# Zero-padding copies on another queue, an earlier projection and a reordered start in a two-branch kernel (long filter beside chunked attention)

## The chip, the cores and the metric

The kernel runs on one core of a Trainium2 chip. The metric is the time of one execution on the device in microseconds. An execution is 8865 instructions on five engines: TensorE (PE in the profile, its weight loads PEld), VectorE (DVE), ScalarE (ACT), GpSimd (POOL) and SyncE (SP), which here only issues DMAs. Each engine takes its instructions in the order in which they were compiled and waits at the first one that isn't ready.

## The reference

Two independent branches work on 2048 tokens by 640 channels in bf16, and their results stand side by side in the output.

Branch A is a gated long filter: a short causal filter of four taps on `k`, times `v`, then a causal convolution of each channel with its own filter of length 2048 (given by Fourier transforms), a skip term, and a gate `q`:

```python
for t in range(ks):                                   # ks = 4
    k_shift = k_shift + k_pad[:, t:t + S, :] * shift_k[:, ks - 1 - t][None, None, :]
kv = k_shift * v
y = irfft(rfft(kv, 2 * S) * rfft(ssm_k, 2 * S))[:S]   # per channel
a = q * (y + kv * ssm_D)
```

Branch B is attention with a memory, 32 heads of width 20, in four segments of 512 tokens:

```python
for s in range(4):
    p = softmax(qs @ ks.T * scale + mask)             # causal within the segment
    a_dot = p @ vs
    a_mem = phi(qs) @ M / (phi(qs) @ z + 1e-6)        # memory of the earlier segments
    outs.append(g * a_mem + (1 - g) * a_dot)
    M = M + phi(ks).T @ vs ; z = z + phi(ks).sum(rows)
b = concat(outs) @ wo                                 # q, k, v = x @ wq, x @ wk, x @ wv
```

## The kernel before

**Branch A** works on five blocks of 128 channels, `dp` 0 to 4 (`a_chunks`). The transforms are matmuls with tables of cosines and sines (`Wf` forward, `Wi` inverse, 1 MB each) between butterflies on DVE. For a block: `load_kv` loads v (`vt`) and transposes k from DRAM into `kr` with four DMA transposes (L184), after a memset of its 16 padding columns on POOL (L182), and makes `skd`, the four taps as diagonal matrices (L186, from `ident` and `skc`). `kshift` (L202) applies the short filter with 64 matmuls and multiplies by v (L203). `fwd` (L218, evicted by ACT in L221) and `bfly` transform the product ("X") and the long filter ("K"). `load_sk` loads the long filter (L169), reorders it on DVE (L171) and transposes it by DMA (L175). Then come `pointwise`, the inverse butterfly `ybfly`, and `inverse` (L283, L284), which stores through POOL (L285).

**Branch B** works in eight units `u`: segment u // 2, half u % 2 of the heads (16 heads, in four groups of four).

- `b_proj_chunks(u)` makes the operands of unit u: `xT` by DMA transpose (L301, once for two units), four chunks `proj(t)` of 128 tokens (L312; ACT copies K and Q into one of two tiles `KQ` in L314, and SP transposes these into `KT` and `QT`, L317 and L318), `bound`, and `mem`, which adds to the memory. `bound` finds the greatest magnitude of K (`kam`, L328, which needs all of KT), makes the positive features of Q (`PqT`, L332 to L335, which needs all of QT), takes magnitudes of Q (`qabs`, L337), multiplies them (L340, `pb`), and writes the result bT as one extra row of each head into QT (four DMAs, L345). That row lowers the scores, so that the exponentials need no maximum.
- `b_attn_chunks(u)` is the attention: two `spread` steps copy KT into the zero-padded tiles `KZ[0]` and `KZ[1]` (L377, four DMAs each, one for a head of each group of four), and four `attn(g)` steps use them: scores (L395), exponentials on ACT (L399), the causal mask on DVE (L402), the product with V (L412), the memory's part (L415) and the normalisation on DVE (L418 to L426). `KZ[0]` serves groups 0 and 1, `KZ[1]` groups 2 and 3. There is one `KT` tile, so the next unit's KT waits until both spreads have read this one. After each second unit comes the output projection (`outt`, `outproj`, L441 to L443).

**The order** is a list of chunks with written costs. `merge` interleaves lists so that each goes forward by the same share of its cost: unit u's attention (28.2 in all) with unit u+1's projection (16 to 17.6) and the output projection of earlier units; then this whole list of B with the list of A. Ahead of it stands a start: the projection of unit 0 and the forward part of block 0. The tile framework turns the list into one instruction order per engine; it follows the list as a priority, by modelled readiness, so the compiled order can differ from the list in detail.

**Queues.** SP issues nearly all DMAs, transposes among them, one after the other. POOL issues constants, `Drow` (the skip weights, L173) and all stores. ACT issues three loads at the start (`bt`, two thirds of `w0`, `Wf`), where `w0` and `w1` are the two halves of the projection weights.

Of the kernel before, what the change touches and what calls it, by code (L numbers as in the profile page):

```python
# [10 lines left out]
BF16_NP = ml_dtypes.bfloat16  # L11
bf16 = mybir.dt.bfloat16
# [48 lines left out]
class K3:  # L61
    def __init__(self, ctx, tc, A_q, A_k, A_v, A_shift_k, A_ssm_k, A_ssm_D, B_x, B_wq, B_wk, B_wv, B_wo, B_beta, out):
        self.tc = tc
        nc = self.nc = tc.nc
# [20 lines left out]
        c = self.consts  # L85
        V = nc.vector

        def const(name, arr, dt):
            t = c.tile(list(arr.shape), dt, name=name)
            nc.gpsimd.dma_start(out=t[:], in_=nc.inline_tensor(arr, name="c_" + name).ap())  # L90
            return t

        self.Wf = c.tile([128, 2, 4, 512], bf16, name="Wf")
# [4 lines left out]
        def wload(engs, half):  # L98
            def f():
                for i, (w, eng) in enumerate(zip((B_wk, B_wq, B_wv), engs)):  # L100
                    eng.dma_start(out=self.wqkv[:, :, half, i, :], in_=w.rearrange("(cc p) j -> p cc j", p=128)[:, :, 320 * half:320 * half + 320])
            return f
        self.deferred = {
            "Wf": lambda: nc.scalar.dma_start(out=self.Wf[:], in_=nc.inline_tensor(Wf_np, name="c_wf").ap()),
            "Wi": lambda: nc.sync.dma_start(out=self.Wi[:], in_=nc.inline_tensor(Wi_np, name="c_wi").ap()),
            "w0": wload((nc.scalar, nc.scalar, nc.sync), 0), "w1": wload((nc.sync,) * 3, 1),
            "wo": lambda: nc.sync.dma_start(out=self.wo[:], in_=B_wo.rearrange("(cc p) j -> p cc j", p=128)),
        }
        self.skc = c.tile([128, 5, 4], bf16, name="skc")
        nc.gpsimd.dma_start(out=self.skc[:], in_=self.shift_k.rearrange("(c p) t -> p c t", p=128))  # L110
        self.ident = const("ident", np.eye(128).astype(BF16_NP), bf16)
        bt = self.bt = c.tile([128, H], bf16, name="bt")
        nc.scalar.dma_start(out=bt[:], in_=B_beta.partition_broadcast(128))
        self.sel = const("sel", sel_np, bf16)
# [44 lines left out]
    def a_chunks(self, dp):  # L159
        nc = self.nc  # L160
        V = nc.vector
        dsl = slice(128 * dp, 128 * dp + 128)
        Wf, Wi, ident = self.Wf, self.Wi, self.ident
# [13 lines left out]
        def load_kv():  # L177
            vt = st["vt"] = io.tile([128, 4, 4, 128], bf16, name="vt", tag="vt")
            for b in range(4):
                nc.sync.dma_start(out=vt[:, b], in_=self.v[512 * b:512 * b + 512, dsl].rearrange("(p c) d -> p c d", c=4))  # L180
            kr = st["kr"] = io.tile([128, 4, KPAD + 512], bf16, name="kr", tag="kr")
            nc.gpsimd.memset(kr[:, :, 0:KPAD], 0.0)  # L182
            for c in range(4):
                nc.sync.dma_start_transpose(out=kr[:, c, KPAD:KPAD + 512], in_=self.k[:, dsl].rearrange("(r c) d -> r c d", c=4)[:, c, :])  # L184
# [9 lines left out]
        def kshift(b):  # L194
            def f():
                kr, vt = st["kr"], st["vt"]
                ps = self.bank(self.ps_a, "pks")
                for c in range(4):
                    for t in range(4):
                        cc = (c - t) % 4  # L200
                        p0 = KPAD + 128 * b + (c - t - cc) // 4
                        nc.tensor.matmul(ps[:, 128 * c:128 * c + 128], lhsT=kr[:, cc, p0:p0 + 128], rhs=st["skd"][:, t, :], start=(t == 0), stop=(t == 3))  # L202
                V.tensor_tensor(out=vt[:, b, :, :], in0=ps[:].rearrange("p (c d) -> p c d", d=128), in1=vt[:, b, :, :], op=ALU.mult)  # L203
            return f
# [69 lines left out]
        def inverse(c):  # L274
# [11 lines left out]
            return f  # L286

        X = [(load_kv, 0.1)] + [(kshift(a), 1.5) for a in range(4)] + [(fwd("X", c), 2.0) for c in range(4)] + [(bfly("X"), 7.0)]
        Kc = [(load_sk, 0.1)] + [(fwd("K", c), 2.0) for c in range(4)] + [(bfly("K"), 5.5)]
        Dl = [(load_q, 0.1), (pointwise(0), 4.6), (pointwise(1), 5.0), (ybfly, 7.6)] + [(inverse(c), 1.7) for c in range(4)]  # L290
        return X + Kc, Dl

    def b_proj_chunks(self, u):
        nc = self.nc
# [71 lines left out]
    def b_attn_chunks(self, u):  # L366
        nc = self.nc
# [5 lines left out]
        def spread(gg):  # L373
            def f():
                for hl in range(4):
                    rows = slice(32 * hl, 32 * hl + DH + 1)
                    nc.sync.dma_start(out=self.KZ[gg][rows, :, hl, :], in_=self.KTs[u][rows, 2 * gg:2 * gg + 2, :])  # L377
            return f

        def attn(g):  # L380
# [67 lines left out]
        tail = [(outt, 0.1)] + [(outproj(t), 1.5) for t in range(4)] if half == 1 else []  # L448
# [1 line left out]


def merge(*lists):
    lists = [l for l in lists if l]
    tot = [sum(c for _, c in l) for l in lists]
    done = [0.0] * len(lists)
    idx = [0] * len(lists)
    out = []
    for _ in range(sum(len(l) for l in lists)):
        best = None
        for i, l in enumerate(lists):  # L460
            if idx[i] < len(l):
                v = (done[i] + 0.5 * l[idx[i]][1]) / tot[i]
                if best is None or v < best[0]:
                    best = (v, i)
        i = best[1]
        out.append(lists[i][idx[i]])
        done[i] += lists[i][idx[i]][1]
        idx[i] += 1
    return out


NST, NA, NB, NO = 3, 2, 2, 1


@with_exitstack
def kernel(
    ctx: ExitStack,
    tc: tile.TileContext,
    A_q: bass.AP,
    A_k: bass.AP,  # L480
    A_v: bass.AP,
    A_shift_k: bass.AP,
    A_ssm_k: bass.AP,
    A_ssm_D: bass.AP,
    B_x: bass.AP,
    B_wq: bass.AP,
    B_wk: bass.AP,
    B_wv: bass.AP,
    B_wo: bass.AP,
    B_beta: bass.AP,  # L490
    out: bass.AP,
):
    K = K3(ctx, tc, A_q, A_k, A_v, A_shift_k, A_ssm_k, A_ssm_D, B_x, B_wq, B_wk, B_wv, B_wo, B_beta, out)
    K.xTs, K.o_s, K.oT, K.KTs = {}, {}, {}, {}
    D_ = K.deferred
    A_ = [K.a_chunks(dp) for dp in range(5)]
    a_pro = A_[0][0]
    a_main = []
    for dp in range(5):
        a_main += merge(A_[dp][1], A_[dp + 1][0] if dp < 4 else [])  # L500
    p0 = K.b_proj_chunks(0)
    seq = [p0[0], (D_["w0"], 0), (D_["Wf"], 0), a_pro[0]] + p0[1:4] + [(K.beta_setup, 0)] + p0[4:5] + merge(p0[5:], a_pro[1:] + [(D_["w1"], 0)])
    seq += [(D_["Wi"], 0), (D_["wo"], 0)]
    b_main = []
    tail = []
    for u in range(8):
        pre, at, nt = K.b_attn_chunks(u)
        main = pre + at
        b_main += merge(main, K.b_proj_chunks(u + 1) if u + 1 < 8 else [], tail)
        tail = nt  # L510
    b_main += tail
    seq += merge(b_main, a_main)
    for ch, _ in seq:
        ch()
# [30 lines left out]
```

## Time and profile before

| | |
|---|---|
| median of 3 runs | 408.53 us (408.29 to 412.5) |
| the profiled execution | 409.29 us, span 407.5 us |
| PE, DVE, ACT, POOL busy | 334.9, 303.1, 281.6, 40.1 us |
| mean granted TensorE clock | 0.908 |
| moved by DMA | 40.95 MB |

An engine's line of the page gives its busy time, the share of the span and the instructions. A group's line gives source line, engine, operation, what it writes and reads, the count, then busy time and mean ns of one, then the idle time just before and what ended it. A line of the timeline gives the start, the busy time (both in us), the engine, the source line, the operation and the count; in brackets stands how long the engine had been idle and what released it. "SPq" and "POOLq" are the issuing queues. The granted clock is the share of full speed that TensorE was given.

### The profile page before, as it was taken

To read this page: it belongs to the slowest core of one execution; us is meant where nothing else is said; L and a number is where in the kernel's file an instruction comes from. 1 tells how busy PE (TensorE), PEld (TensorE's weight loads), DVE (VectorE), ACT (ScalarE), POOL (GpSimd) and SP (SyncE) were. 2 spreads that over 40 slices of the span, in tenths; PEclk is the share of its full clock that TensorE was granted. 3 is DMA by queue.
4 is the path that set the end of the run, shared out by engine and by line. 5 is a ranking of instruction groups with operands and counts; after the bars stand their busy time and mean duration, and the time that the engine had idled before them with its cause. 6 is when DMAs were issued, how large, how long until landed. Compare 5 with 4: busy or idle time off the path is not lost.

```text
span 407.5 us, 8865 instructions
## 1 busy us (share of the span) xinstructions
PE 334.9 (82%) x3453; PEld 224.8 (55%) x3466; DVE 303.1 (74%) x539; ACT 281.6 (69%) x633; POOL 40.1 (10%) x65
## 2 busy tenths in 40 slices
PE   0874989877997889889987999899967999677853
PEld 0552666544674657557764666577734667234632
DVE  0434579689679799984998998799988645899820
ACT  1331597954978379987985799958893897667602
POOL 8400000000011000101000010120000011200021
PEclk9987999968997889989998999999988899866968
DMA  8999257553645354633753364564223422400061
GB/s 209 216 199 279 55 97 140 109 121 71 143 94 120 83 107 75 139 89 69 158 117 73 71 117 70 119 131 92 27 55 43 84 68 57 109 27 1 14 105 64
DMA packets 109594, 40.95 MB, mean 100 GB/s; under 512 B 100144, under 2 KB 107472, under 8 KB 109296
## 3 DMA queue, kind: packets, MB, share of 16 engines
q1 hardware_dynamic: 105872, 33.15, 40.2%
q0 software_dynamic: 2080, 5.36, 5.2%
q10 hardware_dynamic: 1600, 1.88, 1.5%
q8 instruction: 27, 0.44, 0.5%
q14 instruction: 15, 0.12, 0.1%
HBM read 13.36 MB, written 5.24 MB: 46 GB/s over the span
## 4 chain that ended last, share of the span: by engine, by line
issue 39%; PE 26%; ACT 12%; DVE 8%; SPq 5%; DMA 4%; POOL 4%; POOLq 0%; DVEq 0%; ACTq 0%
ACT ET L399 7%; PE kqv L312 7%; PE stp L395 5%; PE pf L218 5%; DMA KT<-KQ 3%; PE po L412 3%; ACT F L221 2%; POOL out_dram L285 2%; SPq L180 2%; PE pb L340 2%; POOL out_dram L443 1%; PE pks L202 1%; PE py L283 1%; SPq L184 1%; DMA QT<-KQ 1%
## 5 line engine op out<-in xcount | busy, mean ns | idle before, releaser
L399 ACT ACTIVATE ET<-stp 128x512 bf16<-128x512 f32 (+1 forms) x384 | 173.5, 552 | 21.8 <-PE stp L395 17.8
L395 PE MATMUL stp<-QT,KZ 128*128 128x128 bf16 (+3 forms) x499 | 120.7, 324 | 18.6 <-ACT ET L399 14.7
L312 PE MATMUL kqv<-wqkv,xT 128*128 128x320 bf16 x480 | 86.5, 317 | 15.7 <-DMA xT<-in_B_x_dram 9.6
L395 PEld LDWEIGHTS <-KZ 128*128 128x128 bf16 x512 | 50.7, 104 | 52.9 <-issue 36.3
L312 PEld LDWEIGHTS <-xT 128*128 128x128 bf16 x480 | 47.3, 103 | 37.0 <-DMA xT<-in_B_x_dram 9.6
L221 ACT CAST F<-pf 128x512 bf16<-128x512 f32 x80 | 45.7, 616 | 20.4 <-PE pf L218 18.6
L412 PEld LDWEIGHTS <-ET 128*128 128x128 bf16 x1280 | 41.5, 97 | 26.2 <-DVE ET L402 14.2
L412 PE MATMUL po<-Va,ET 128*128 128x21 bf16 x1280 | 44.5, 174 | 11.4 <-DVE ET L402 7.1
L402 DVE TENSOR_TENSOR ET<-ET,cmask 128x1024 bf16<-128x1024 bf16 x64 | 41.8, 685 | 13.2 <-ACT ET L399 13.1
L314 ACT CAST KQ<-kqv 128x320 bf16<-128x320 f32 x64 | 28.4, 460 | 29.4 <-PE kqv L312 24.8
L218 PEld LDWEIGHTS <-Wf 128*128 128x128 bf16 x320 | 30.4, 101 | 26.1 <-issue 19.2
L441 PE MATMUL pfo<-wo,oT 128*128 128x320 bf16 x160 | 32.3, 323 | 4.0 <-DMA oT<-o_s 4.0
L218 PE MATMUL pf<-vt,Wf 128*128 128x256 bf16 x160 | 27.3, 294 | 9.4 <-DVE vt L203 8.7
L218 PE MATMUL pf<-kT,Wf 128*128 128x256 bf16 x160 | 27.0, 281 | 4.2 <-ACT F L221 4.0
L418 DVE RECIPROCAL rr<-po 128x16 f32<-128x16 f32 (+1 forms) x64 | 15.5, 242 | 14.9 <-PE po L415 10.1
L328 DVE TENSOR_REDUCE kam<-KT 128x4 f32<-128x2048 bf16 x8 | 18.3, 2284 | 10.4 <-DMA KT<-KQ 9.5
L285 POOL DMA_DIRECT2D out_dram<-outa x20 | 15.1, 758 | 99.5 <-DVE outa L284 69.1
L202 PE MATMUL pks<-skd,kr 128*128 128x128 bf16 x320 | 24.7, 225 | 0.0
L283 PE MATMUL py<-S,Wi 128*128 128x256 bf16 x160 | 23.4, 272 | 1.3 <-DVE outa L284 0.9
L314 ACT CAST Va<-kqv 128x320 bf16<-128x320 f32 x32 | 14.0, 438 | 14.6 <-PE kqv L312 8.3
L442 ACT CAST outb<-pfo 128x320 bf16<-128x320 f32 x32 | 13.5, 472 | 15.1 <-PE pfo L441 13.8
L425 DVE TENSOR_TENSOR o<-po,rr 128x320 bf16<-128x320 f32 x48 | 23.2, 484 | 0.3
(78 smaller groups left out, 405.0 us busy)
## 6 DMA issues: line engine op xcount, KB each, us to landing
KZ<-KT SPq DMA_DIRECT2D x64, 42.0 KB
vt<-in_A_v_dram SPq DMA_DIRECT2D x20, 128.0 KB
sk<-in_A_ssm_k_dram SPq DMA_DIRECT2D x5, 512.0 KB
qd<-in_A_q_dram SPq DMA_DIRECT2D x20, 128.0 KB
out_dram<-outa POOLq DMA_DIRECT2D x20, 128.0 KB, 3.2
out_dram<-outb POOLq DMA_DIRECT2D x16, 160.0 KB, 2.1
Wf<-c_wf ACTq DMA_DIRECT2D x1, 1024.0 KB
Wi<-c_wi SPq DMA_DIRECT2D x1, 1024.0 KB
```

Of the source, the lines that this page charges most:

```text
L202: nc.tensor.matmul(ps[:, 128 * c:128 * c + 128], lhsT=kr[:, cc, p0:p0 + 128], rhs=st["skd"][:, t, :], start=(t == 0), stop=(t == 3))
L218: nc.tensor.matmul(o, lhsT=Wf[:, h, c, 256 * i + 128 * j:256 * i + 128 * j + 128], rhs=rhs, start=(h == 0), stop=(h == 1 and not last))
L221: nc.scalar.copy(out=F[:, c, i, :], in_=pf[:])
L283: nc.tensor.matmul(pyv[:, :, h, :], lhsT=Wi[:, k, c, 128 * h:128 * h + 128], rhs=U[:, 4 * i + c, 256 * j:256 * j + 256], start=(k == 0), s ...
L285: nc.gpsimd.dma_start(out=self.out[:, dsl].rearrange("(b p c) d -> p c b d", b=4, c=4)[:, c], in_=outa[:])
L312: nc.tensor.matmul(kq[:, 0:320], lhsT=xT[:, cc, tok], rhs=self.wqkv[:, cc, half, i, :], start=(cc == 0), stop=(cc == 4))
L314: nc.scalar.copy(out=dst, in_=kq[:, 0:320].rearrange("p (h d) -> p h d", d=DH))
L395: nc.tensor.matmul(sts[j][:, c0:c0 + n], lhsT=KZ[:, g % 2, hl, 128 * kc:128 * kc + 128], rhs=QT[:, g, 128 * kc:L], start=True, stop=True)
L399: nc.scalar.activation(out=ET[:, 2 * hp + j, e0:e0 + width], in_=sts[j][:, 0:width], func=ACTF.Exp, scale=SCALE)
L402: V.tensor_tensor(out=blk, in0=blk, in1=self.cmask[:, None, None, :].to_broadcast([128, 4, 2, 128]), op=ALU.mult)
L412: nc.tensor.matmul(ops[:, qc % 2, hl, 0:DH + 1], lhsT=ET[:, hl, c0:c0 + 128], rhs=Va[:, kc, 4 * g + hl, 0:DH + 1], start=(kc == 0), stop=( ...
L441: nc.tensor.matmul(pf[:, 0:320], lhsT=oT[:, cc, 128 * tci:128 * tci + 128], rhs=self.wo[:, cc, 320 * i:320 * i + 320], start=(cc == 0), st ...
```

## The change

- The `spread` copies into KZ are issued from POOL's queue (`nc.gpsimd`) instead of SP's.
- `merge` takes a list with a span: the next unit's projection is laid out so that it ends when 0.6 (`PW`) of the current unit's attention list has gone by. Before, it ended with the attention.
- The start is reordered: the long filter's load and block 0's loads come first, then `xT` and `w0`, then the short filter, then the K transform merged with projections 0 and 1, then the X transform merged with the rest of unit 0's projection, its bound and its memory. For block 0 the K part stands ahead of the X part.
- At the start some loads change queues: v of block 0 and the third part of `w0` go to ACT's queue, `skc` and `ident` from POOL's to SP's.

The instructions of the engines stay the same in number and shape.

```diff
-            nc.gpsimd.dma_start(out=t[:], in_=nc.inline_tensor(arr, name="c_" + name).ap())
+            eng.dma_start(out=t[:], in_=nc.inline_tensor(arr, name="c_" + name).ap())
...
-            "w0": wload((nc.scalar, nc.scalar, nc.sync), 0), "w1": wload((nc.sync,) * 3, 1),
+            "w0": wload((nc.scalar,) * 3, 0), "w1": wload((nc.sync,) * 3, 1),
...
-        nc.gpsimd.dma_start(out=self.skc[:], in_=self.shift_k.rearrange("(c p) t -> p c t", p=128))
-        self.ident = const("ident", np.eye(128).astype(BF16_NP), bf16)
+        nc.sync.dma_start(out=self.skc[:], in_=self.shift_k.rearrange("(c p) t -> p c t", p=128))
+        self.ident = const("ident", np.eye(128).astype(BF16_NP), bf16, nc.sync)
...
-                nc.sync.dma_start(out=vt[:, b], in_=self.v[512 * b:512 * b + 512, dsl].rearrange("(p c) d -> p c d", c=4))
+                (nc.scalar if dp == 0 else nc.sync).dma_start(out=vt[:, b], in_=self.v[512 * b:512 * b + 512, dsl].rearrange("(p c) d -> p c d", c=4))
...
-        return X + Kc, Dl
+        return (X + Kc if dp else Kc + X), Dl
...
-                    nc.sync.dma_start(out=self.KZ[gg][rows, :, hl, :], in_=self.KTs[u][rows, 2 * gg:2 * gg + 2, :])
+                    nc.gpsimd.dma_start(out=self.KZ[gg][rows, :, hl, :], in_=self.KTs[u][rows, 2 * gg:2 * gg + 2, :])
...
 def merge(*lists):
-    lists = [l for l in lists if l]
-    tot = [sum(c for _, c in l) for l in lists]
+    lists = [l if isinstance(l, tuple) else (l, 1.0) for l in lists]
+    spans = [w for l, w in lists if l]
+    lists = [l for l, w in lists if l]
+    tot = [sum(c for _, c in l) / w for l, w in zip(lists, spans)]
...
+PW = 0.6
...
-    seq = [p0[0], (D_["w0"], 0), (D_["Wf"], 0), a_pro[0]] + p0[1:4] + [(K.beta_setup, 0)] + p0[4:5] + merge(p0[5:], a_pro[1:] + [(D_["w1"], 0)])
+    ld_k, fk, ld_v, ks, fx = a_pro[0], a_pro[1:6], a_pro[6], a_pro[7:11], a_pro[11:]
+    seq = [ld_k, (D_["Wf"], 0), ld_v, p0[0], (D_["w0"], 0)] + ks
+    seq += merge(fk, p0[1:3]) + [(K.beta_setup, 0)] + merge(fx, p0[3:] + [(D_["w1"], 0)])
     seq += [(D_["Wi"], 0), (D_["wo"], 0)]
...
-        b_main += merge(main, K.b_proj_chunks(u + 1) if u + 1 < 8 else [], tail)
+        b_main += merge(main, (K.b_proj_chunks(u + 1) if u + 1 < 8 else [], PW), tail)
```

More of the change, by code (lines that the diff above doesn't have):

```diff
@@ L86, in __init__, with const @@
         V = nc.vector
-        def const(name, arr, dt):
+        def const(name, arr, dt, eng=nc.gpsimd):
             t = c.tile(list(arr.shape), dt, name=name)
-            nc.gpsimd.dma_start(out=t[:], in_=nc.inline_tensor(arr, name="c_" + name).ap())
+            eng.dma_start(out=t[:], in_=nc.inline_tensor(arr, name="c_" + name).ap())
             return t
```

## The prediction

> **What bounds the kernel now.** I read the page first, then the windows of the head, the middle and the end, then the places where TensorE stood.
>
> ```profile
> span 407.5 us, 8865 instructions
> PE 334.9 (82%) x3453; PEld 224.8 (55%) x3466; DVE 303.1 (74%) x539; ACT 281.6 (69%) x633; POOL 40.1 (10%) x65
> PEclk9987999968997889989998999999988899866968
> ```
>
> ```profile
> 55.00:345.00 290.00, 258.67 (x2826) 178.21 (x2837) 238.92 (x430) 230.56 (x522) 18.15 (x31) 0.94 0.46 94
> 345.00:407.50 62.50, 40.70 (x388) 23.67 (x386) 42.71 (x71) 31.87 (x70) 7.76 (x12) 0.79 0.24 55
> 0.00:55.00 55.00, 35.49 (x244) 22.91 (x245) 21.45 (x39) 19.19 (x42) 14.19 (x23) 0.91 0.83 188
> ```
>
> Columns of a window: length, then busy time of PE, PEld, DVE, ACT, POOL with counts, then granted clock, DMA share, GB/s. No engine is full over the span, and the three stages differ: TensorE has 89% of the middle (258.67 of 290), 65% of the head and of the end. Where it idles it also loses clock. So I use one measure for a stretch, its **loss**: length minus PE busy times clock. The head loses 55 − 35.49 × 0.91 = 22.7 us. In the middle the loss sits in a few places:
>
> ```profile
> 80.00:100.00 20.00, 13.59 (x143) 8.31 (x143) 17.81 (x32) 10.22 (x23) 0.00 (x0) 0.76 0.43 97
> 125.00:150.00 25.00, 20.11 (x211) 13.48 (x212) 22.50 (x34) 14.84 (x30) 0.90 (x2) 0.80 0.43 99
> 170.00:180.00 10.00, 7.65 (x78) 4.39 (x77) 9.49 (x18) 9.58 (x20) 1.07 (x2) 0.83 0.58 138
> 210.00:225.00 15.00, 11.64 (x129) 7.48 (x129) 12.26 (x20) 10.59 (x25) 0.15 (x1) 0.89 0.37 87
> 300.00:320.00 20.00, 14.40 (x105) 7.95 (x106) 17.64 (x31) 12.48 (x27) 0.00 (x0) 0.74 0.33 59
> 230.00:300.00 70.00, 66.53 (x758) 47.08 (x762) 63.32 (x110) 60.11 (x139) 5.74 (x9) 1.00 0.49 93
> ```
>
> Losses: 9.7, 8.9, 3.7, 4.6 and 9.3, together 36.2 us in 90 us. The quiet stretch 230 to 300 loses 3.5 of 70, 5%; at that rate 90 us would lose 4.5. The excess is 31.7 us. All five stretches are boundaries between two units (a unit is 512 tokens by 16 heads). The last boundary shows the mechanism:
>
> ```profile
> 343.48 1.22 SPq L318 DMA_TRANSPOSE QT<-KQ  x1
> 344.76 2.29 DVE L328 TENSOR_REDUCE kam<-KT 128x4 f32<-128x2048 bf16 x1 [0.30 <-DMA KT<-KQ]
> 346.01 1.91 ACT L332 ACTIVATE PqT<-QT 128x2048 bf16<-128x2048 bf16 x1 [2.47 <-DMA QT<-KQ]
> 347.69 0.69 DVE L334 TENSOR_SCALAR tq<-QT 128x2048 bf16<-128x2048 bf16 x1
> 348.89 1.22 DVE L335 TENSOR_TENSOR PqT<-PqT,tq 128x2048 bf16<-128x2048 bf16 x1
> 350.15 0.69 DVE L337 TENSOR_SCALAR qabs<-QT 128x2048 int16<-128x2048 int16 x1
> 353.19 0.57 ACT L342 CAST bT<-pb 16x512 bf16<-16x512 f32 x1 [1.22 <-PE pb L340]
> 353.79 2.60 SPq L345 DMA_DIRECT2D QT<-bT  x4
> 356.50 1.74 SPq L377 DMA_DIRECT2D KZ<-KT  x2
> 359.34 0.81 PE L395 MATMUL stp<-QT,KZ 128*128 128x512 bf16 x3
> ```
>
> The next unit's first score matmul starts 15.9 us after the last projection's QT transpose is issued (343.48 to 359.34). Between them lie the maximum kam, qabs, the bound matmuls, bT, four row copies and the zero-padding copies KZ. The exponentials have nothing to do meanwhile; with ACT L399 alone (busy, clock, DMA):
>
> ```profile
> 310.00:315.00 5.00, 0.00 (x0) 1.00 0.48 55
> 355.00:360.00 5.00, 0.24 (x1) 1.00 0.17 53
> ```
>
> Moreover ACT stood 2.47 us for QT with exponentials queued behind it.
>
> **The change part by part.**
>
> *PW = 0.6.* By merge's costs, the bound of the next unit moves from just ahead of attn(3) to ahead of attn(2) of the current one. After it lie two attention groups. L399's row (below) has 173.5 us for 32 groups, 5.4 us each, so 10.8 us of exponentials stand against the 15.9 us chain, with work of the filter branch among them: the chain is mostly covered. What stays is the standing in ACT and DVE for the transposes: in both orders at most one attention group separates the last projection from its bound, for units 6 and 7 none. I take half of the excess: **−16 us**, with bounds 25% (−8) and all (−32). What is next late is DVE, 63.3 of 70 busy in the quiet stretch.
>
> *The end.* Of the last bound, DVE's kam, tq, PqT and qabs (2.29 + 0.69 + 1.22 + 0.69 = 4.9 us) leave a full stretch for one that is half empty:
>
> ```profile
> 320.00:340.00 20.00, 19.88 (x224) 13.65 (x223) 8.89 (x21) 18.38 (x46) 1.85 (x3) 1.00 0.25 57
> 345.00:390.00 45.00, 32.87 (x348) 19.04 (x346) 42.02 (x70) 28.56 (x62) 4.82 (x7) 0.81 0.17 41
> ```
>
> DVE has 42.0 of 45 us after 345, where pointwise and inverse butterfly lie in both orders, so little more than these ops can go: **−5 us**, bounds 0 and −8.
>
> *The head.* Now and in the parts that move:
>
> ```profile
> 0.74 3.28 SPq L301 DMA_TRANSPOSE xT<-in_B_x_dram  x1
> 1.30 0.99 POOL L110 DMA_DIRECT2D skc<-in_A_shift_k_dram  x1 [0.86 <-POOLq L529]
> 2.29 0.56 POOL L90 DMA_DIRECT2D ident<-c_ident  x1
> 9.59 2.85 PE L312 MATMUL kqv<-wqkv,xT 128*128 128x320 bf16 x10 [9.59 <-DMA xT<-in_B_x_dram]
> 12.46 5.29 SPq L184 DMA_TRANSPOSE kr<-in_A_k_dram  x4
> 14.04 0.17 POOL L182 MEMSET kr<- 128x64 bf16 x1
> 24.27 0.84 PE L312 MATMUL kqv<-wqkv,xT 128*128 128x320 bf16 x5 [2.58 <-ACT KQ L314]
> 37.30 1.65 PE L218 MATMUL pf<-vt,Wf 128*128 128x256 bf16 x7 [6.02 <-DVE vt L203]
> ```
>
> TensorE starts at 9.59, with the projection. After the change it starts with the short filter, which needs kr's padding, set by POOL behind its constants and its long memsets. Two POOL DMAs leave ahead of it (0.99 + 0.56), so 14.04 + 0.17 − 1.55 = 12.7: 3.1 us later. The four kr transposes are covered: from 0.74, three SP issues (taken as 0.6 each, near ident's 0.56) and 5.29 end at 7.8. xT now comes behind them: issued 7 us later, it would land at about 9.59 + 7 = 16.7, and the 64 filter matmuls (24.7 us for 320 in the page's row, so 4.9 for 64) fill 12.7 to 17.6. w0 shares the DMA engines with Wf and v, and the last weight may be later still. Against that stand the two holes inside the head, 2.58 and 6.02: with the K transforms between the projections TensorE has other work there. 3.1 − 8.6 = −5.5; **−5 us**, bounds −10 (also the clock part, 35.49 × 0.09 = 3.2, goes) and +4 (the holes stay). v, skc, ident and w0's third load change queues; each is one issue of about 0.6 us on SP or ACT before any compute of theirs, so nothing.
>
> *KZ on Pool, and the crowding.*
>
> ```profile
> L377 SPq DMA_DIRECT2D KZ<-KT x64: 762/796/1112, 34.7 to 357.4; - x64
> L399 ACT ACTIVATE ET<-stp 128x512 bf16<-128x512 f32 (+1 forms) x384 | 173.5, 552 | 21.8 <-PE stp L395 17.8
> L202 PE MATMUL pks<-skd,kr 128*128 128x128 bf16 x320 | 24.7, 225 | 0.0
> L285 POOL DMA_DIRECT2D out_dram<-outa x20 | 15.1, 758 | 99.5 <-DVE outa L284 69.1
> out_dram<-outa POOLq DMA_DIRECT2D x20, 128.0 KB, 3.2
> ```
>
> SP loses 64 issues of 0.80, 6.4 us per unit; the transposes behind them go out sooner (in the half counted above). Pool gets them. Pool shows no such copy: nearest are its stores at 0.76 us and 3.2 us to landing; bounds 0.5 (ident's) and 1.0 (skc's). A spread of four then takes 4 × 0.76 + 3.2 = 6.2 us. It waits as before for KZ to be free, and the next unit's KT transposes wait for it, because there is one KT tile. What is new is how soon something needs them: with proj(2) now ahead of attn(1), ACT's copy into the reused KQ half stands until proj(0)'s two transposes are through, and exponentials queue behind it. 6.2 + 2 × 1.2 (transposes) + 2.5 (landing, as in the 2.47 wait) = 11.1 us into a unit, where proj(2) comes after attn(0) and two projections, 10 us or more. Behind a waiting spread on Pool stand the output stores, the one-row load Drow and the padding memset of the next kr; DVE's outa has two buffers, so a short wait reaches nobody. I put 0.7 us on each of seven units: **+5 us**, bounds 0 and the +35 of the last rival.
>
> On the port: the Trainium skill, "SBUF — State Buffer", "Who interferes with whom", says that a DMA from Pool can stand still while DVE holds the shared port in a two-port mode; an example on that page, 620 against 3100 ns, would add by estimate 2.5 us to an issue, 20 us to a unit's eight. The trace's 20 Pool stores, at DVE 90% busy, average 0.76 us, which speaks against it here.
>
> Sum: −5 − 16 − 5 + 5 = −21. The profiled execution took 409.29 us, so 388.3; the median of 408.53 is 0.8 lower: **388 us**. Its own range: with three quarters of the excess and the head at −10, 409.3 − 24 − 10 − 5 + 5 = 375; with a quarter and the head at +4, 405.
>
> **The rivals.**
>
> *All the excess goes.* −32 for the boundaries, −10 for the head, −5 for the end, nothing added: 362; with three quarters of it and the head at −5, 375. For: the chain is a latency, no engine's work. Against: DVE at 90% in the quiet stretch. Chance 0.13.
>
> *The gain is taken back.* TensorE or DVE is full in every quiet stretch, so holes moved out of the boundaries return elsewhere, and the compiled order need not follow the list:
>
> ```profile
> 69.62 1.15 SPq L184 DMA_TRANSPOSE kr<-in_A_k_dram  x1
> ```
>
> This kr is block 2's, listed near the last attention group of the second unit, and it went out before the first boundary at 80. So the span of 0.6 may not be what the engines see. Only the head or the end remains: 409 − 5 = 404. Chance 0.17.
>
> *Slower: the spread comes late.* Pool is in order and stands most of the time in front of a store that waits for its data (99.5 us ahead of 20 stores, 5 us each). A spread queued behind one is late by that, and with it KT's transposes, the KQ halves and ACT. With 5 us in each of seven units, 35 us stand in place of my +5: 409.3 − 26 + 35 = 418. It turns slower once a unit loses more than 26 / 7 = 3.7 us. The port stall that the Trainium skill names would work through the same place. Chance 0.20.
>
> **How the numbers follow.** A measurement of this kernel tells about 1% from no change: 404.4 to 412.6. The forecast has 0.50. Faster: 0.50 + 0.13 + a third of the taken-back case, 0.06 = 0.69; slower: 0.19 of the late spread's 0.20; the rest, 0.12, is the same. The range 370 to 414 leaves out half of the first rival (0.06) and two thirds of the late spread (0.13), 0.2 together.
>
> **What would show it.** Windows of L399 without empty 5 us slices at the boundaries, and PE clock near 1.00 there; loss of the head under 20 us, first matmul (L202) near 12.7; the last unit's first score matmul within 3 us of the previous unit's last exponential; KZ on Pool near 0.76 us. I am wrong if ACT's wait for KT grows beyond its few us, if Pool's KZ issues wait long behind stores, if PE's first matmul comes after 16, or if the exponentials' empty slices stay.

## The result, and the profile after

The changed kernel takes **392.73 us** (median of four runs, 389.64 to 394.48), the kernel before 409.1 beside it: a ratio of 0.958, 95% interval 0.949 to 0.966. The forecast was 388, its range 370 to 414. The profiled execution took 391.97 us, and its numbers are used below.

From the page of the changed kernel, first the span, TensorE's line and the granted clock by slices; then the group of the zero-padding copies, and their DMA line (KB each, us from issue to landing):

```profile
span 390.0 us, 8955 instructions
PE 326.1 (84%) x3466; PEld 222.3 (57%) x3466; DVE 302.2 (77%) x539; ACT 279.6 (72%) x633; POOL 80.1 (21%) x127
PEclk9999869999999989899998999899999999999588
...
L377 POOL DMA_DIRECT2D KZ<-KT x64 | 39.8, 624 | 131.2 <-PE stp L395 62.0
...
KZ<-KT POOLq DMA_DIRECT2D x64, 42.0 KB, 2.3
```

POOL counts 62 instructions more: the 64 copies have come, and the issues of `skc` and `ident` have gone. The mean clock is 0.949 (0.908 before; over the runs on record 0.905 to 0.925 before and 0.949 to 0.969 in the changed kernel). TensorE's idle time went from 407.5 − 334.9 = 72.6 us to 63.9, and its matmuls took 8.8 us less, at the higher clock: half of the 17.5 us each. (Of before, 13 of 3466 matmul records are missing, all of L395. At 0.32 us each its idle time is up to 4 us too great, so up to 4 us of the first half may belong to the second.)

The clearest division of the span is by the first exponential of each unit. Three windows of the kernel before (from the start to unit 0's first exponential, from there to unit 7's first, and the rest), then the same three of the changed kernel; columns as in the prediction:

```profile
0.00:54.70 54.70, 35.19 (x242) 22.69 (x243) 21.45 (x39) 18.89 (x41) 14.19 (x23) 0.91 0.83 188
54.70:359.80 305.10, 267.32 (x2905) 182.75 (x2916) 252.62 (x447) 238.29 (x538) 20.72 (x34) 0.93 0.46 94
359.80:407.50 47.70, 32.35 (x310) 19.35 (x309) 29.00 (x54) 24.44 (x56) 5.19 (x8) 0.75 0.19 40
```

```profile
0.00:62.60 62.60, 38.63 (x316) 28.42 (x317) 31.39 (x48) 19.41 (x44) 19.16 (x30) 0.92 0.91 205
62.60:341.60 279.00, 254.12 (x2798) 173.55 (x2797) 239.62 (x436) 235.85 (x534) 54.62 (x88) 0.98 0.45 91
341.60:390.00 48.40, 33.31 (x355) 20.37 (x353) 31.16 (x57) 24.34 (x57) 6.36 (x10) 0.83 0.25 57
```

Units 0 to 6 gained 26.1 us (305.1 to 279.0), the head lost 7.9, the end lost 0.7: together −17.5. Of the 26.1 us, 12.9 are TensorE's idle time (305.10 − 267.32 = 37.8 us to 24.9) and 13.2 its busy time, of which 3.4 us went into the head and 1.0 into the end.

**The boundaries** did what the prediction asked of them. Windows of the changed kernel around three of the seven:

```profile
85.00:100.00 15.00, 13.66 (x154) 8.41 (x153) 13.88 (x29) 14.77 (x38) 2.97 (x5) 1.00 0.26 56
...
168.00:183.00 15.00, 14.78 (x179) 10.68 (x178) 10.60 (x27) 11.07 (x26) 3.21 (x6) 1.00 0.25 63
...
335.00:350.00 15.00, 13.39 (x164) 8.32 (x163) 13.91 (x26) 14.60 (x36) 5.08 (x8) 1.00 0.33 88
```

Clock 1.00 and at most 1.6 us of idle in 15. The other four have clock 1.00 as well; the most idle of them, 120 to 140, has 3.4 us in 20. Before, the five stretches that the prediction named had clocks of 0.74 to 0.89. From a unit's last exponential to the next unit's first the seven gaps were 65.9 us in sum and are 20.1. TensorE was not idle for all of that time. The sums over the seven gaps, before and after:

```profile
sum 65.90, PE 52.51 PEld 36.62 DVE 56.22 ACT 25.11 POOL 4.06; mean PE 7.50 PEld 5.23 DVE 8.03 ACT 3.59 POOL 0.58
...
sum 20.20, PE 19.72 PEld 14.90 DVE 18.66 ACT 10.74 POOL 6.30; mean PE 2.82 PEld 2.13 DVE 2.67 ACT 1.53 POOL 0.90
```

It stood for 13.4 us of the 65.9 and stands for 0.5 of the 20.2. The difference, 12.9 us, is the whole fall of TensorE's idle time in the units (up to 4 us of it may be the missing records). The last boundary, in the timeline of the changed kernel:

```profile
324.10 1.19 SPq L318 DMA_TRANSPOSE QT<-KQ  x1
324.99 2.29 DVE L328 TENSOR_REDUCE kam<-KT 128x4 f32<-128x2048 bf16 x1 [0.73 <-DMA KT<-KQ]
325.71 2.47 POOL L377 DMA_DIRECT2D KZ<-KT  x4 [3.66 <-PE pf L218]
331.93 0.57 ACT L342 CAST bT<-pb 16x512 bf16<-16x512 f32 x1 [0.49 <-PE pb L340]
332.53 2.45 SPq L345 DMA_DIRECT2D QT<-bT  x4
...
341.07 0.81 PE L395 MATMUL stp<-QT,KZ 128*128 128x512 bf16 x4
```

From the last QT transpose to the scores it is no shorter (17.0 us, it was 15.9). But the last row copy has left SP by 334.98, 10.9 us after the transpose (12.9 before), and the scores at 341.07 show no wait for it: TensorE was still at unit 6's work. Unit 6's last exponential ends at 341.1, and unit 7's first stands at 341.6.

**The head** went the other way. The stretch from 40 to 50 us, of before and then, with lines of its timeline, of after:

```profile
40.00:50.00 10.00, 9.96 (x75) 6.24 (x73) 4.18 (x6) 5.18 (x11) 0.50 (x1) 0.86 0.22 71
```

```profile
40.00:50.00 10.00, 1.99 (x32) 1.75 (x31) 3.77 (x3) 0.49 (x1) 2.60 (x4) 0.81 0.86 183
...
39.76 1.25 SPq L192 DMA_DIRECT2D qd<-in_A_q_dram  x2
41.06 0.63 SPq L169 DMA_DIRECT2D sk<-in_A_ssm_k_dram  x1
41.79 1.72 SPq L317 DMA_TRANSPOSE KT<-KQ  x1
...
47.37 2.28 DVE L328 TENSOR_REDUCE kam<-KT 128x4 f32<-128x2048 bf16 x1
47.40 5.37 POOL L377 DMA_DIRECT2D KZ<-KT  x8 [21.69 <-DMA KT<-KQ]
50.43 1.88 PE L340 MATMUL pb<-qabs,A 128*16 128x512 bf16 x4 [8.39 <-DVE A L330]
```

Unit 0's last KT transpose stands on SP behind three loads of block data, and at a DMA share of 0.86 it lands at 47.40, 5.6 us after its issue. Only then can kam begin, and TensorE has nothing left but the bound that needs it: a hole of 8.39 us. The kernel before had its hole earlier: from 30 to 40 us TensorE worked 3.98 us, and now works 9.24; from 30 to 60 it is 22.85 us before and 20.80 after. The start did put more work ahead (38.63 us of matmuls before the first exponential against 35.19). In matmuls of branch A (L202, L218, L220, L283) it is 194 against 125, and unit 0 has some 60 fewer.

### The profile page after: what moved, and what is told of

It reads as the page before. It is cut to its first block, busy times and chain, and to the rows that moved or that the text cites. A ratio compares the mean times of both kernels' runs of the same rounds, so it can differ in the third digit from the quotient of the medians.

```text
span 390.0 us, 8955 instructions
## 1 busy us (share of the span) xinstructions
PE 326.1 (84%) x3466; PEld 222.3 (57%) x3466; DVE 302.2 (77%) x539; ACT 279.6 (72%) x633; POOL 80.1 (21%) x127
## 4 chain that ended last, share of the span: by engine, by line
PE 44%; ACT 23%; issue 14%; DMA 9%; DVE 5%; SPq 3%; POOL 2%; POOLq 0%; DVEq 0%; ACTq 0%
ACT ET L399 16%; PE kqv L312 13%; PE stp L395 7%; PE po L412 5%; PE pf L218 5%; PE pfo L441 4%; ACT F L221 3%; PE pks L202 3%; DMA QT<-KQ 3%; DMA xT<-in_B_x_dram 2%; DMA KT<-KQ 2%; PE py L283 2%; PE pb L340 2%; SPq L184 2%; ACT PqT L332 1%
## 5 line engine op out<-in xcount | busy, mean ns | idle before, releaser
L399 ACT ACTIVATE ET<-stp 128x512 bf16<-128x512 f32 (+1 forms) x384 | 172.3, 560 | 15.8 <-PE stp L395 12.6
L395 PE MATMUL stp<-QT,KZ 128*128 128x512 bf16 (+3 forms) x512 | 116.3, 306 | 15.5 <-ACT ET L399 11.4
L312 PE MATMUL kqv<-wqkv,xT 128*128 128x320 bf16 x480 | 82.9, 305 | 1.2 <-DMA xT<-in_B_x_dram 0.9
L395 PEld LDWEIGHTS <-KZ 128*128 128x128 bf16 x512 | 48.2, 99 | 51.0 <-issue 36.0
L377 POOL DMA_DIRECT2D KZ<-KT x64 | 39.8, 624 | 131.2 <-PE stp L395 62.0
L312 PEld LDWEIGHTS <-xT 128*128 128x128 bf16 x480 | 45.7, 99 | 21.3 <-issue 2.9
L412 PEld LDWEIGHTS <-ET 128*128 128x128 bf16 x1280 | 42.1, 97 | 14.5 <-DVE o L425 5.3
L202 PE MATMUL pks<-skd,kr 128*128 128x128 bf16 x320 | 28.0, 241 | 17.4 <-DMA kr<-in_A_k_dram 13.1
L218 PEld LDWEIGHTS <-Wf 128*128 128x128 bf16 x320 | 30.5, 99 | 17.6 <-issue 9.3
L202 PEld LDWEIGHTS <-kr 128*128 128x128 bf16 x320 | 23.6, 109 | 21.3 <-DMA kr<-in_A_k_dram 13.3
L441 PE MATMUL pfo<-wo,oT 128*128 128x320 bf16 x160 | 28.8, 314 | 5.8 <-DMA oT<-o_s 5.3
L442 ACT CAST outb<-pfo 128x320 bf16<-128x320 f32 x32 | 13.3, 451 | 23.4 <-PE pfo L441 20.3
L218 PE MATMUL pf<-kT,Wf 128*128 128x256 bf16 x160 | 26.3, 279 | 4.1 <-ACT F L221 2.7
L418 DVE RECIPROCAL rr<-po 128x16 f32<-128x16 f32 (+1 forms) x64 | 15.5, 243 | 14.4 <-PE po L415 10.9
L283 PE MATMUL py<-S,Wi 128*128 128x256 bf16 x160 | 24.9, 287 | 2.0 <-DVE outa L284 2.0
L218 PE MATMUL pf<-vt,Wf 128*128 128x256 bf16 x160 | 24.5, 279 | 2.2 <-ACT F L221 1.5
L441 PEld LDWEIGHTS <-oT 128*128 128x128 bf16 x160 | 15.6, 101 | 13.6 <-DMA oT<-o_s 6.1
```

The lines of the kernel that those rows point to most:

```text
L218: nc.tensor.matmul(o, lhsT=Wf[:, h, c, 256 * i + 128 * j:256 * i + 128 * j + 128], rhs=rhs, start=(h == 0), stop=(h == 1 and not last))
L283: nc.tensor.matmul(pyv[:, :, h, :], lhsT=Wi[:, k, c, 128 * h:128 * h + 128], rhs=U[:, 4 * i + c, 256 * j:256 * j + 256], start=(k == 0), s ...
L312: nc.tensor.matmul(kq[:, 0:320], lhsT=xT[:, cc, tok], rhs=self.wqkv[:, cc, half, i, :], start=(cc == 0), stop=(cc == 4))
L377: nc.gpsimd.dma_start(out=self.KZ[gg][rows, :, hl, :], in_=self.KTs[u][rows, 2 * gg:2 * gg + 2, :])
L395: nc.tensor.matmul(sts[j][:, c0:c0 + n], lhsT=KZ[:, g % 2, hl, 128 * kc:128 * kc + 128], rhs=QT[:, g, 128 * kc:L], start=True, stop=True)
L399: nc.scalar.activation(out=ET[:, 2 * hp + j, e0:e0 + width], in_=sts[j][:, 0:width], func=ACTF.Exp, scale=SCALE)
```

## The experiments

Each kernel was timed beside the kernel before. The ratio is given with its 95% interval. "Span", "Pool" and "start" are the three parts of the change. The table divides the profiled execution of each kernel by the first exponentials of the units, read off the L399 rows of the timelines; "gaps" is the sum of the seven stretches between a unit's last exponential and the next one's first, "idle" is span minus TensorE's busy time (up to 4 us too great where 10 to 13 matmul records are missing: in all rows but "after", "span + start" and "start + Pool", which have them all). Where an edit adds lines to kernel.py, the line numbers of that run shift by as many. All in us.

| kernel | head | U0 | U1 | U2 | U3 | U4 | U5 | U6 | U7, end | gaps | idle |
|---|---|---|---|---|---|---|---|---|---|---|---|
| before | 54.7 | 43.1 | 47.0 | 44.5 | 43.2 | 39.9 | 44.9 | 42.5 | 47.7 | 65.9 | 72.6 |
| after | 62.6 | 30.4 | 37.5 | 49.9 | 39.6 | 46.6 | 36.8 | 38.2 | 48.4 | 20.1 | 63.9 |
| span only | 54.3 | 39.5 | 40.8 | 54.8 | 39.6 | 46.9 | 36.8 | 39.8 | 48.2 | 23.4 | 74.1 |
| Pool only | 54.0 | 39.0 | 46.5 | 45.6 | 40.0 | 41.3 | 43.7 | 44.2 | 46.3 | 66.7 | 70.7 |
| start only | 60.8 | 38.8 | 42.5 | 45.7 | 44.6 | 39.7 | 45.3 | 42.5 | 47.6 | 67.4 | 76.3 |
| span + Pool | 54.6 | 38.1 | 39.8 | 55.2 | 39.7 | 48.0 | 36.8 | 38.6 | 48.7 | 22.5 | 69.7 |
| span + start | 61.3 | 38.1 | 37.7 | 51.4 | 37.7 | 47.5 | 36.8 | 39.2 | 49.1 | 20.5 | 69.7 |
| start + Pool | 61.3 | 35.8 | 41.9 | 44.9 | 43.8 | 39.9 | 45.7 | 43.2 | 46.3 | 61.9 | 72.4 |
| span + Pool, kr held | 55.9 | 38.2 | 39.9 | 53.5 | 37.8 | 45.7 | 36.8 | 40.2 | 46.3 | 22.6 | 68.2 |
| after, 0.8 | 61.1 | 33.2 | 41.6 | 45.2 | 40.8 | 38.6 | 39.5 | 42.1 | 46.8 | 48.5 | 67.6 |
| after, 0.45 | 62.6 | 31.1 | 40.2 | 47.5 | 48.0 | 49.5 | 33.3 | 37.2 | 46.9 | 24.3 | 72.7 |

### Each part alone

**Span only**, from the kernel before (the new `merge`, and):

```diff
-        b_main += merge(main, K.b_proj_chunks(u + 1) if u + 1 < 8 else [], tail)
+        b_main += merge(main, (K.b_proj_chunks(u + 1) if u + 1 < 8 else [], PW), tail)
```

> The kernel before with one part of the change: the next projection laid out to end at 0.6 of the current attention. Theory: this part carries the gain, by taking the bound's chain out of the boundaries, so 389 to 395 us and empty exponential stretches gone from most boundaries. Rival one, the SP queue: without the copies leaving SP the transposes stay late, so 400 to 408. Rival two, the start carries the gain: 404 to 412.

Measured: 400.91 us, 0.980 (0.973 to 0.987). This is the rival's number, not the theory's. The gaps close as in the full change (23.4 us), so the span does what it says; but unit 2 becomes 10.3 us longer, the others 17.2 shorter together, and TensorE's idle time doesn't fall at all (74.1). What is gained is busy time, 326.6 us against 334.9, at a clock of 0.952.

**Pool only**, from the kernel before:

```diff
-                    nc.sync.dma_start(out=self.KZ[gg][rows, :, hl, :], in_=self.KTs[u][rows, 2 * gg:2 * gg + 2, :])
+                    nc.gpsimd.dma_start(out=self.KZ[gg][rows, :, hl, :], in_=self.KTs[u][rows, 2 * gg:2 * gg + 2, :])
```

> The kernel before with the KZ copies on Pool's queue alone. Theory: the copies were not what was late last (the row bT was), so 405 to 411, no change. Rival one, the SP queue: SP freed of 6.4 us a unit brings the transposes sooner, 395 to 402. The late-spread rival of the prediction: 412 to 418.

Measured: 402.93 us, 0.984 (0.979 to 0.990), 6.3 us better by the medians. "No change" falls, and the queue theory comes nearer, though its 395 to 402 isn't reached. The gaps stay as they were (66.7 us), so the gain lies elsewhere. One place shows in the timelines: the last of unit 0's eight copies had left SP at 60.1 us and leaves Pool at 40.0, and unit 0 is 4.1 us shorter. That this is the relief of SP fits, but no run freed SP without moving the copies.

**Start only**, from the kernel before: the reordered `seq`, the K part ahead for block 0, and the loads that change queues, as in the diff of the change; the span stays 1.

> The kernel before with the reordered start and its changed queues alone. Theory, from the hole of 8.4 us that the profile after shows in front of the bound matmuls of unit 0: the start now costs 3 to 6 us, so 412 to 415. Rival two: the start gains as the prediction had it, 5 us, so 403 to 405.

Measured: 408.06 us, 0.997 (0.993 to 1.000). Neither number came: the start alone is worth nothing that can be told apart. The table says why. The first exponential comes 6.1 us later, units 0 and 1 are 8.8 us shorter, since some 70 of the filter's matmuls have gone from them into the head, units 2 and 3 give 2.6 back, and from unit 4 on the first exponentials stand within 0.3 us of where they stood before.

### Each part taken out

**Span + Pool**: the changed kernel with the start and the loads of the kernel before.

> The changed kernel with the old start: the projection's span of 0.6 and the copies on Pool only. Theory: 386 to 390, faster than the changed kernel by the 3 to 6 us that the start costs. Rival two: 396 to 400, slower than the changed kernel by the start's 5 us.

Measured: 401.31 us, 0.979 (0.973 to 0.984), above both ranges, and the theory had the sign wrong. So the start, worth nothing alone, is worth 2.1% of the time (some 8.6 us) in company.

**Span + start**: the changed kernel with `nc.sync` in the copies into KZ.

> The changed kernel with the KZ copies back on SP's queue: the span of 0.6 and the reordered start. Theory now, after the parts alone gave 0.980 (span), 0.984 (Pool), 0.997 (start) and span with Pool only 0.979: span and Pool take away the same waits, so taking Pool away again costs little, 392 to 397. Rival: the start gives its gain only with Pool's queue, since SP is the start's bottleneck; then 399 to 405.

Measured: 399.75 us, 0.980 (0.976 to 0.984): the rival's range, though the number alone doesn't show the rival's reason. Pool is worth 2.2% in company.

**Start + Pool**: the changed kernel with

```diff
-PW = 0.6
+PW = 1.0
```

> The changed kernel with the projection spread over the whole attention again (a span of 1.0): reordered start and Pool's queue. Theory: without the span the chain of the bound stands at the boundaries again; the start adds little, as alone, so 398 to 403. Rival, the start and Pool are what works together: 391 to 396.

Measured: 404.61 us, 0.992 (0.989 to 0.995). The theory's range ends 1.6 us below it, so the span is worth even more in company than was expected, 3.4%.

Put together, by the ratios: span −2.0%, Pool −1.6%, start −0.3% alone; span + Pool −2.1%, span + start −2.0%, start + Pool −0.8%; all three −4.2%. A pair gives about what its better part gives, or less; the three together give about the sum of the singles (3.9%), within the interval. Beside the two others each part is worth 2 to 3.4%, alone 0.3 to 2.0%: no fixed price can be charged to a part.

### What a late spread costs

**Each copy into KZ is issued twice**, otherwise the changed kernel:

```diff
-                    nc.gpsimd.dma_start(out=self.KZ[gg][rows, :, hl, :], in_=self.KTs[u][rows, 2 * gg:2 * gg + 2, :])
+                    for _ in range(2):
+                        nc.gpsimd.dma_start(out=self.KZ[gg][rows, :, hl, :], in_=self.KTs[u][rows, 2 * gg:2 * gg + 2, :])
```

> The changed kernel with each KZ copy issued twice on Pool, so that a spread is 2.4 us later and Pool issues 128 of them. It tests the prediction's slower rival, that a late spread holds KT, the KQ halves and ACT. Theory: a spread has that much slack, so no more than 3 us over the changed kernel, 391 to 396. The rival: each of seven units loses about 2.4 us, 408 to 411.

Measured: 401.53 us, 0.986 (0.979 to 0.993), 2.9% above the changed kernel: between the two. Its waits (total, times, longest):

```profile
POOL KZ L378 <- DMA KZ<-KT: 41.6, 30, 3.1
...
ACT KQ L314 <- DMA KT<-KQ: 3.4, 2, 2.9
```

The doubling is more than an issue: the second copy also waits for the first to land. The spreads come later by 64 × 0.62 us of issues and these 41.6 us, together 81 in eight units, 10 us each over its two spreads; the time rises by 8.8 us by the medians and 11.7 by the ratios, 1.1 to 1.5 a unit. That is a mean: in the profile 4.3 of the 8.9 us fall in unit 0 (34.7 us against 30.4). Late spreads cost, but a ninth to a seventh of their lateness, and ACT's wait for KT is a small part of it. The run also moves 2.8 MB more and keeps Pool longer from its stores, and it doesn't tell these from the lateness.

### The hole of the head

**Late tables**: the changed kernel, in which the loads of `Wi` and `wo` (the inverse transform's and the output's tables) are held until unit 0's bT is there, by two small POOL copies from bT into a corner of each table that the load then writes over:

```diff
+            if u == 0:
+                nc.gpsimd.tensor_copy(out=self.Wi[0:16, 0, 0, 0:1], in_=bT[:, 0:1])
+                nc.gpsimd.tensor_copy(out=self.wo[0:16, 0, 0:1], in_=bT[:, 0:1])
```

> The changed kernel with the two loads of the inverse table Wi and of wo, 1.85 MB, held back until unit 0's bound row bT is there (two small Pool copies write a corner of each tile first, which makes the loads wait). It tests what makes the hole of 8.4 us in the new start. Theory: KT's last transposes land late because the DMA queue is full of loads that nothing needs yet; then KT lands some 4 us sooner, the hole shrinks to 2 to 5 us, and the time is 387 to 391. Rival: the order on SP and DVE alone makes the hole (loads for block 1 ahead of KT's last transposes and the maximum kam behind the reordering copy); then it stays over 6 us and the time is 391 to 395.

Measured: 391.71 us, 0.960 (0.956 to 0.965): not to be told from the changed kernel. The stretch and the bound in its profile:

```profile
40.00:50.00 10.00, 7.02 (x61) 4.79 (x61) 5.21 (x8) 4.70 (x11) 3.54 (x5) 0.84 0.73 150
...
40.02 0.43 ACT L314 CAST KQ<-kqv 128x320 bf16<-128x320 f32 x1 [3.72 <-DMA KT<-KQ]
...
48.90 1.03 PE L340 MATMUL pb<-qabs,A 128*16 128x512 bf16 x4 [2.00 <-DVE A L330]
```

The last KT transpose now lands 3.1 us after its issue (42.74 to 45.83) in place of 5.6. The wait ahead of the bound fell from 8.39 to 2.00 us, a wait of 3.72 for KT came up earlier, and the first exponential is 2.8 us sooner (59.8). So the theory had the hole: loads that nothing needs yet are a cause of it. It hadn't the time, which is the rival's: the end doesn't show the gain, and what was late in the head is made up in the units.

### Unit 2

In the kernels with the span but without the start, unit 2 is 10.3 to 10.7 us longer than before. In the timeline of span + Pool:

```profile
137.44 5.11 SPq L184 DMA_TRANSPOSE kr<-in_A_k_dram  x4
142.65 5.63 SPq L432 DMA_TRANSPOSE oT<-o_s  x4
145.33 2.85 PE L441 MATMUL pfo<-wo,oT 128*128 128x320 bf16 x10 [4.92 <-DMA oT<-o_s]
150.03 0.24 DVE L426 TENSOR_TENSOR o_s<-o 128x160 bf16<-128x160 bf16 x1 [6.93 <-DMA oT<-o_s]
```

The four transposes of segment 0's output (one tile `o_s`, one tile `oT`) stand on SP behind block 3's four K transposes, which became free to go at about the same time, and VectorE and TensorE wait. In the changed kernel the same two waits are 2.2 and 2.0 us. Two runs hold the K transposes of block 3 back until oT has landed, by a one-column copy into kr:

```diff
+            if dp == 3:
+                nc.gpsimd.tensor_copy(out=kr[:, :, KPAD:KPAD + 1], in_=self.oT[0][:, 0:4, L - 1:L])
```

**Span + Pool, kr held:**

> The kernel with the longer span and the copies on Pool, in the old order of the start (401.3 us), in which the four K transposes of block 3 are made to wait until the output transposes of the first segment have landed, by a one-column Pool copy from the transposed output into the K tile. Theory (what the longer span loses in unit 2 is a queue: the output transposes of the first segment stand on SP behind block 3's K transposes, and VectorE's o_s and TensorE's output projection wait for them): the waits of 6.93 us (o_s for the output transposes) and 4.92 us (output projection for them) go below 2.5 us, the stretch from unit 2's first exp to unit 3's falls from 55.2 us to about 50, and the time is 395 to 398 us. Rival (the stretch is long because the work of the projection is packed into it, and the queue only shows it): the two waits go, others take their place, and the time stays at 400 to 402 us. A second rival (block 3's K now comes too late): its shift or its projection waits, over 402 us.

Measured: 396.93 us, 0.972 (0.966 to 0.977), inside the theory's times. But the theory's place is wrong. In its profile, whose line numbers are two further on:

```profile
138.75 6.04 SPq L434 DMA_TRANSPOSE oT<-o_s  x4
146.33 0.24 DVE L428 TENSOR_TENSOR o_s<-o 128x160 bf16<-128x160 bf16 x1 [1.76 <-DMA oT<-o_s]
...
ACT KQ L316 <- DMA KT<-KQ: 4.2, 1, 4.2
...
PE kqv L314 <- ACT KQ L316: 4.0, 2, 3.4
```

The waits went as expected, unit 2 is shorter by only 1.7 us (53.5, not about 50), and within it the projection now waits 4 us for KT and KQ, as the rival said. The other 3.5 us of the span lie elsewhere. Against span + Pool the ratio is 0.7% lower, with intervals that overlap: a small gain at most.

**Late tables, kr held:**

> The changed kernel with the late loads of the start's tables moved behind unit 0's work (391.7 us) and block 3's K transposes held behind the output transposes of the first segment, as in the run beside it. Theory of the queue: the waits for the output transposes are only 2.2 us here already, so the gain is small: 387 to 390 us. Rival (nothing left to gain there): 391 to 392 us.

Measured: 394.3 us, 0.966 (0.961 to 0.971). No gain; the rival's 391 to 392 is nearest. So the queue of unit 2 explains a small part, at most, of what the start is worth in company; the rest stays open. Where it lies can be read off the table: against span + Pool the changed kernel loses 8.0 us in the head and gains 15.3 in units 0 to 2.

### The size of the span

The changed kernel with `PW` 0.8, and with 0.45:

> The changed kernel with 0.8 instead of 0.6 as the span of the next projection. Theory (0.6 empties the boundaries, whose gaps sum to 20 us of 278; what is between 0.6 and 1 opens them again): boundary gaps sum to 35 to 45 us, 395 to 401 us. Rival (the time follows the order that results more than the span): 390 to 394 us.

> The changed kernel with 0.45 instead of 0.6. Theory (the gaps at the boundaries are nearly gone at 0.6, and a shorter span packs the same work into the first half of each attention, where TensorE has no more room): 394 to 400 us, with the time between exps longer inside the units and gaps below 15 us in sum. Rival (the order that results decides): 388 to 392 us.

Measured: 391.68 us, 0.962 (0.958 to 0.966) with 0.8; 398.92 us, 0.980 (0.974 to 0.986) with 0.45. For 0.45 the theory's time came, but not its gaps (24.3 us, not below 15); for 0.8 it failed, and the rival's number came. With 0.8 the gaps are open again, 48.5 us in sum; the exponentials (L399) alone, in four slices of its profile (length, ACT busy, clock, DMA share, GB/s), then all engines around three boundaries:

```profile
125.00:130.00 5.00, 0.00 (x0) 1.00 0.61 152
130.00:135.00 5.00, 0.00 (x0) 1.00 0.35 67
175.00:180.00 5.00, 0.00 (x0) 1.00 0.36 87
213.00:218.00 5.00, 0.00 (x0) 1.00 0.04 10
...
120.00:140.00 20.00, 15.74 (x199) 11.30 (x200) 18.50 (x32) 10.19 (x24) 3.35 (x6) 0.91 0.40 88
168.00:183.00 15.00, 14.72 (x178) 11.00 (x178) 9.25 (x23) 11.22 (x25) 3.33 (x6) 0.96 0.25 60
210.00:225.00 15.00, 14.20 (x144) 9.32 (x144) 13.52 (x25) 11.36 (x26) 1.75 (x3) 0.99 0.31 63
```

The exponentials stand again at the boundaries, and TensorE is busy through two of the three at clocks of 0.96 and 0.99: of the 48.5 us of gaps it stands for 6.9. The time is that of 0.6. With 0.45 the gaps are small and the time is 6 to 7 us longer. So the gaps between the exponentials are no measure of the time: in the table kernels with gaps of 20 to 24 us take from 392.7 to 401.3.

## Why the prediction was right, and where it was not

The time lay 4.7 us above the forecast and well inside the range; the case "faster" came. That the sum came so near is partly luck: the units did 15.1 us better than the −11 forecast for them (−16 and +5), the head 12.9 worse than its −5, the end 5.7 worse than its −5. Step by step:

**Boundaries, −16 (−8 to −32): the gaps closed as forecast, but the term is undersized, it is not the span's alone, and it rests on a misread price.** In the full change the units took 26.1 us less, and −16 with the +5 for KZ makes −11. With the span alone it is −6.9 (298.2 against 305.1): −17.2 in six units, close to the −16, and +10.3 in unit 2. That the holes return elsewhere was my second rival, and for the span alone it holds: idle 72.6 before, 74.1 with it. Its 404 wasn't reached because the clock rose, which I had priced only inside the loss of the boundaries.

What was misread is what a boundary costs. The chain kept the exponentials waiting; TensorE worked through most of that. At the gaps from 179.8 to 189.3 and from 265.1 to 272.4 us it was busy 9.45 of 9.50 and 7.25 of 7.30 us at clock 1.00 before any change. The second of these lies inside the stretch that I called quiet, 170 to 180 ends where the first begins, and the last boundary, whose lines I showed, is in none of the five stretches. At that one TensorE waited longest for VectorE's normalisation of unit 6, and not for the row or for KZ:

```profile
358.55 0.46 PE L412 MATMUL po<-Va,ET 128*128 128x21 bf16 x12 [3.49 <-DVE o L425]
```

The scores behind it, at 359.34, show no wait of their own. So the latency of the chain was not what TensorE's time hung on there.

**The end, −5: wrong, by counting twice.** From unit 7's first exponential on, the kernel takes 48.4 us (47.7 before), and VectorE works 31.16 us of it (29.00). The operations of the last bound stand ahead of that first exponential in both orders. Taking them away from the last boundary was already in the −16.

**The head, −5 (−10 to +4): wrong place, and the wrong sign within the head.** I priced TensorE's start and the two holes I could see. The first filter matmuls came at 10.50 us (12.7 forecast), but only two of them; the next stood until 13.46, and the projection began at 18.81 (16.7). What came last ahead of the bound was unit 0's last KT transpose, and for that I hadn't asked which loads would stand ahead of it on SP or be under way beside it. It cost 7.9 us at the first exponential, loss 62.60 − 38.63 × 0.92 = 27.1 where I asked for under 20. Yet the start is worth nothing alone and 2.1% in company, and mending the hole changed the time by nothing that can be told: the head's own loss isn't what its reordering does to the time. It changes how much filter work is left for the units after it; why that is worth more in company stays open.

**KZ on Pool, +5 (0 to +35): wrong sign.** Pool's copy takes 0.62 us to issue and 2.3 to land, where I took 0.76 and 3.2. The part is worth −6.3 us alone and 2.2% in company. I had put the relief of SP into the boundaries' half and charged Pool the crowding; the net is a gain, and the sign by which I was to be wrong, ACT's wait for KT, went down (4.3 to 1.4 us). That "a short wait reaches nobody" is too strong: 10 us of lateness a unit cost 1.1 to 1.5. The rival of the late spread had a real mechanism, but at this rate it needs 25 to 34 us of lateness a unit for its 3.7.

**The port.** The Trainium skill ("SBUF — State Buffer", "Who interferes with whom") says that a DMA from Pool can stand still while VectorE holds the shared port in a two-port mode. The traces agree with it. The prediction set it aside by the mean of 20 stores, and a mean doesn't show it: the copies' mean issue took 0.62 us, less than SP's 0.80, but some took longer. First the row of the copies in the changed kernel (shortest, median and longest, in ns), then the longest issue with Pool only, and what VectorE did beside it:

```profile
L377 POOL DMA_DIRECT2D KZ<-KT x64: 604/611/1073, 47.4 to 340.8; - x64
...
254.47 1.53 POOL L377 DMA_DIRECT2D KZ<-KT  x1 [0.35 <-PE stp L395]
254.67 1.22 DVE L171 COPY skp<-sk 128x2048 bf16<-128x2048 bf16 x1
```

The issue ends 0.11 us after the copy. In all the kernels that issue the KZ copies on Pool, 28 issues take more than 0.67 us. Each of them lies beside a VectorE COPY or TENSOR_SCALAR and ends 0.11 us after it; in which mode these ran, the traces don't say. The price was small because such meetings are rare here: in the changed kernel 58 of the 64 issues met neither operation (mean 0.61 us, longest 0.65), and two were delayed, by 0.5 and 0.1 us, where the prediction's estimate was 2.5 us for each.

**The loss as a measure.** Busy time times clock, summed over the three windows, is 304.9 us before and 312.2 after, for the same matmuls. The two should be equal; they differ by 7.3 us (up to 4 of it the missing records). So a loss is off by a few us, and the excess of 31.7 had that much uncertainty from the start.

**What would show it:** clock 1.00 at the boundaries and the last unit's first scores at the previous unit's last exponential (341.07 against 341.1) both came; most empty slices went. But the run with 0.8 shows that these are companions of the gain and not its cause. TensorE's idle time and clock are nearer to it: 63.9 to 67.6 us idle in the changed kernel and with 0.8, 72.7 with 0.45. (Idle and busy time make up the span, so this says where the time lies and not why.)

## What to carry to other kernels

Count the idle time of the engine that bounds the kernel, not the gaps of the engine that feeds on it: a gap that work of another branch fills costs nothing, and closing it can open a hole one unit later. For each step that is moved, list what stands ahead of its DMAs on the issuing queue at the new place, and which loads will be under way beside them; here that moved the hole of the head and the waits of unit 2. And where a list is interleaved by a planner, parts of a change don't add: take each part out of the whole as well as trying it alone.

## What the runs showed of the hardware that I hadn't expected

A DMA transpose that lands about 2.5 us after its issue in the middle of the kernel (KT, 322.54 to 324.99 us) took 5.6 in the head at a DMA share of 0.86 (40 to 50 us), and 3.1 there with the tables' loads held back, at 0.73.

A VectorE copy that takes 1.23 us elsewhere took 4.39 beside POOL memsets. From the timeline of the changed kernel, and the group in the kernel before:

```profile
3.48 6.98 POOL L126 MEMSET KZ<- 128x4096 bf16 x2
9.35 4.39 DVE L171 COPY skp<-sk 128x2048 bf16<-128x2048 bf16 x1 [0.38 <-DMA sk<-in_A_ssm_k_dram]
10.38 0.80 POOL L130 MEMSET KQ<- 128x384 bf16 x2
...
11.89 0.76 POOL L134 MEMSET Mbd<- 128x352 bf16 x2
```

```profile
L171 DVE COPY skp<-sk 128x2048 bf16<-128x2048 bf16 x5 | 6.1, 1226 | 9.1 <-PE pf L218 4.9 <-DMA sk<-in_A_ssm_k_dram 4.2
```

This first copy takes 3.85 to 4.39 us in all nine kernels with the new start; in those with the old one it comes later, behind the memsets, and the mean is 1.2. In the nine it begins between 9.35 and 9.91 us and ends between 13.73 and 13.76, whenever it began: 1.1 us after the last of the memsets, which ends at 12.65 in the lines above. That looks as if the copy stood until the whole row of memsets was through and only then ran. It is an inference, since no run moved the memsets.
